# Sparse attention and FFN: the sparse units of each batch's last group take 128 rows instead of 64

## The chip, the cores and the metric

The kernel runs on one core of one Trainium2 chip. The metric is the device time of one execution in microseconds (us). Three executions of the kernel before took 803.14, 804.76 and 806.10 us; the median, 804.76 us, stands for it.

## The reference

Block-sparse attention for 4 batches, 8 heads, 768 positions and head size 64 is followed by a feed-forward net on 3072 tokens of width 512 with 2048 hidden units, all in float32. A query block of 32 positions sees its neighbours, the first and the last key block and three sampled blocks; the first and the last query block see every key.

```python
scores = scale * np.matmul(q, k.transpose(0, 1, 3, 2))
mask = np.abs(blk_i - blk_j) <= window            # blocks of 32, window 1
mask = mask | (blk_i == 0) | (blk_j == 0) | (blk_i == n_blocks - 1) | (blk_j == n_blocks - 1)
for qb in range(n_blocks):
    for kb in sampled_blocks[qb]:
        mask[qb * block:(qb + 1) * block, kb * block:(kb + 1) * block] = True
scores = np.where(mask, scores, -1000000000.0)
attn = np.exp(scores - np.max(scores, axis=-1, keepdims=True))
attn = attn / (np.sum(attn, axis=-1, keepdims=True) + 1e-09)
out = np.matmul(attn, v)

h = x @ w_in                                      # x: the attention's output, 3072 x 512
g = np.maximum(h, 0.0) + np.log1p(np.exp(-np.abs(h)))
return g @ w_out
```

## The kernel before

**Attention.** The 24 query blocks of a batch are dealt into 6 groups of 4 blocks, in the order 1 to 23 and then 0. In the last group only blocks 21 and 22 are sparse; 23 and 0 see every key and form a *whole* set of their own. A batch is so 7 sets (`sets`): five sparse ones, the whole one, and the sparse one of the last group, which comes last. A set is two units (`units`), `a` = 0 and 1, each with two head pairs `j`; a pair is the heads `r` = 0 and 1, which lie in the two halves of the partitions of `q` and `k`. In all there are 56 units, of which 8 are sparse units of a last group.

A sparse unit runs through these stages. `scores` multiplies each of the `ni` query blocks (4, in the last group 2) with its 8 gathered key blocks (256 columns): query block `i` writes the 32 rows from 32*i of the PSUM tile `s` (L622), and DVE scales, masks and takes the row maximum, one instruction per head (L628). `exponents` is one ScalarE activation per head with its row sum (L678). `transposes` turns the probabilities on TensorE in chunks of 128 columns (L691) and copies them out of PSUM, one copy per four chunks, on ScalarE and VectorE (L698, L696). `values` multiplies with the gathered values, query block by query block, 32 rows of the PSUM tile `x` at a time (L721). After a set's second unit `normalise` divides by the row sums (L749 to L751), and `turn` transposes the result on TensorE (L766), from where ScalarE writes the rounded part (`x_high`, L780) and VectorE the rest (`x_low`, L784) into the FFN's input. With `ni` = 2 the score rows, the activations, the transposes and the products use 64 of the 128 rows.

**FFN.** It runs in two phases. Phase 0 takes hidden slices 0 to 5 for 8 blocks of 384 tokens and is mixed into the attention: `hidden` (L255 to L257, 12 products of 384 columns), the softplus on ScalarE and VectorE, `project` (L313 to L315, 9 products of 512 columns). Phase 1 takes slices 6 to 15 for 6 blocks of 512 tokens after the attention.

**Order.** The program lists the pieces of the attention and of the FFN in a fixed interleaving (`pieces`, `due`), in which a unit's scores stand two units ahead of its values. SyncE keeps that order. The other engines' queues are ordered by a list scheduler which works from the program's dependencies and its own estimates; each engine then works through its queue in order. Key blocks are gathered by GpSimd, VectorE and ScalarE copies (`kg`, L530, L516, L497) out of one batch's keys `kT`, which the next batch's replace once the whole set's scores have been taken; GpSimd also starts the indirect loads of sampled values (L588) and adds up the FFN's weights (L187).

## Time and profile before

| | |
|---|---|
| device time, three executions | 803.14, 804.76, 806.10 us (median 804.76) |
| span of the profiled execution, first to last instruction | 802.7 us (its own device time is not listed apart) |
| TensorE matmul busy | 775.1 us, 97% |
| TensorE weight loads | 612.0 us, 76% |
| VectorE busy | 529.6 us, 66% |
| ScalarE busy | 534.1 us, 67% |
| GpSimd busy | 217.2 us, 27% |
| last transposes of the attention | 418 us after the start |

Rows of the timeline give start and duration in us, the engine (PE is TensorE's products, DVE VectorE, ACT ScalarE, POOL GpSimd), the line, the operation, out<-in, and how many instructions the row sums up; in square brackets stands the idle time ahead of the row with what ended it. Neighbouring products overlap, so the cost of a row on TensorE is read from its start to the start of the next row, not from its duration. A product of two float32 operands leaves two records, which is why 8 products of L622 are listed as x16; a transpose leaves one.

### The profile page before, as it was taken

The numbers are of one execution on the slowest core, as the hardware profiler recorded it, in microseconds if no ns is written. First come the engines' busy times: TensorE is split into PE (matmuls) and PEld (weight loads), VectorE is DVE, ScalarE is ACT, GpSimd is POOL, SyncE is SP. The second block draws the span as 40 slices with busy tenths as digits, with TensorE's granted clock in tenths as the row PEclk, the third lists the DMA queues.
The fourth block names the chain that finished last, engine by engine and source line by source line (L and its number), as shares of the span: only waits on it lengthen the run. The fifth ranks groups of instructions, "written<-read, shape, count | busy, mean of one in ns | idle before, by whom it ended". The sixth has DMA issues, their size and how long they took to land.

```text
span 802.7 us, 20684 instructions
## 1 busy us (share of the span) xinstructions
PE 775.1 (97%) x7868; PEld 612.0 (76%) x7868; DVE 529.6 (66%) x1266; ACT 534.1 (67%) x1210; POOL 217.2 (27%) x389
## 2 busy tenths in 40 slices
PE   8779999999999999999999999999999999999997
PEld 8556777877777777787788888888888888888886
DVE  5779998888768768785656765454454544644544
ACT  5878997778777777777666775555555555555552
POOL 6864886526456355552000000000000000000000
PEclk9999999999999999999999999999999999999999
DMA  8899998877986976856315950320330412300301
GB/s 250 246 237 320 250 265 225 263 249 237 226 283 193 292 254 189 243 168 220 121 41 185 311 186 2 105 105 1 105 105 17 139 56 92 118 1 1 105 0 53
DMA packets 59731, 129.60 MB, mean 161 GB/s; under 512 B 5553, under 2 KB 17969, under 8 KB 58609
## 3 DMA queue, kind: packets, MB, share of 16 engines
q1 hardware_dynamic: 53632, 109.79, 44.2%
q0 software_dynamic: 5712, 17.57, 7.9%
q8 instruction: 62, 1.02, 0.5%
q10 hardware_dynamic: 288, 0.93, 0.3%
q14 instruction: 37, 0.29, 0.1%
HBM read 97.85 MB, written 30.41 MB: 160 GB/s over the span
## 4 chain that ended last, share of the span: by engine, by line
PE 68%; DVE 13%; ACT 11%; DMA 4%; issue 3%; SPq 1%; POOL 0%; POOLq 0%; DVEq 0%; ACTq 0%
PE h L255 9%; PE o L313 9%; PE h L256 9%; PE h L257 9%; PE o L314 9%; PE o L315 9%; ACT pr L678 4%; PE x L721 3%; PE t L691 3%; PE s L622 3%; DVE pr L628 2%; PE warm L853 2%; DVE e L268 2%; DVE wt L183 1%; DMA x<-xD 1%
## 5 line engine op out<-in xcount | busy, mean ns | idle before, releaser
L268 DVE SCALAR_TENSOR_TENSOR e<-u,e 128x512 f32<-128x512 f32 (+1 forms) x108 | 76.2, 705 | 184.5 <-ACT u L266 184.2
L255 PE MATMUL h<-x,w 128*128 128x512 f32 (+1 forms) x432 | 163.4, 378 | 3.2 <-DVE e L269 2.3
L256 PE MATMUL h<-x,w 128*128 128x512 f32 (+1 forms) x432 | 159.2, 369 | 0.0
L257 PE MATMUL h<-x,w 128*128 128x512 f32 (+1 forms) x432 | 159.0, 368 | 0.0
L313 PE MATMUL o<-w,gh 128*128 128x512 f32 x384 | 155.6, 405 | 0.0
L314 PE MATMUL o<-w,gh 128*128 128x512 f32 x384 | 152.5, 397 | 0.0
L315 PE MATMUL o<-w,gl 128*128 128x512 f32 x384 | 151.8, 395 | 0.0
L259 ACT ACTIVATE e<-h 128x512 f32<-128x512 f32 (+1 forms) x108 | 59.2, 548 | 132.2 <-PE h L257 132.0
L678 ACT ACTIVATE pr<-pr,nmax 128x256 f32<-128x256 f32 (+2 forms) x208 | 110.0, 530 | 30.7 <-DVE nmax L628 18.5
L588 POOL DMA_INDIRECT vg<-in_v_dram,ix x88 | 87.9, 998 | 73.7 <-PE x L721 43.1
L255 PEld LDWEIGHTS h<-x,w 128*128 128x128 f32 x432 | 81.1, 188 | 20.5 <-DVE e L269 2.9
L530 POOL COPY kg<-kT 128x128 f32 x252 | 84.8, 381 | 43.9 <-PE s L622 41.1
L313 PEld LDWEIGHTS o<-w,gh 128*128 128x128 f32 x384 | 72.1, 188 | 24.8 <-issue 8.6
L257 PEld LDWEIGHTS h<-x,w 128*128 128x128 f32 x432 | 81.2, 188 | 10.7
L256 PEld LDWEIGHTS h<-x,w 128*128 128x128 f32 x432 | 81.3, 188 | 10.5
L283 ACT CAST gh<-u 128x512 fp32r<-128x512 f32 (+1 forms) x108 | 61.5, 569 | 41.5 <-PE o L314 41.1
L315 PEld LDWEIGHTS o<-w,gl 128*128 128x128 f32 x384 | 72.1, 188 | 17.7 <-issue 0.4
L314 PEld LDWEIGHTS o<-w,gh 128*128 128x128 f32 x384 | 72.2, 188 | 16.2 <-issue 0.8
L274 ACT ACTIVATE u<-u 128x512 f32<-128x512 f32 (+1 forms) x108 | 62.9, 582 | 24.8 <-DVE e L268 24.6
L628 DVE CUSTOM_DVE_ANT_1 pr<-s,mask 128x256 f32<-128x256 f32 (+1 forms) x192 | 69.4, 414 | 6.4 <-PE s L622 6.4
L289 DVE TENSOR_TENSOR gl<-u,gh 128x512 fp32r<-128x512 f32 (+1 forms) x108 | 70.1, 649 | 4.9 <-ACT gh L283 4.5
L279 DVE TENSOR_TENSOR u<-u,e 128x512 f32<-128x512 f32 (+1 forms) x108 | 69.8, 646 | 3.5 <-ACT u L274 1.6
(81 smaller groups left out, 1072.3 us busy)
## 6 DMA issues: line engine op xcount, KB each, us to landing
vg<-in_v_dram SPq DMA_DIRECT2D x19, 768.0 KB, 6.8
xD<-x SPq DMA_DIRECT2D x8, 1536.0 KB, 11.1
raw<-in_w_in_dram SPq DMA_DIRECT2D x16, 512.0 KB, 10.7
raw<-in_w_out_dram SPq DMA_DIRECT2D x16, 512.0 KB, 10.4
qc<-in_q_dram SPq DMA_DIRECT2D x24, 256.0 KB, 8.7
vg<-in_v_dram SPq DMA_DIRECT2D x12, 512.0 KB, 4.7
yD<-os SPq DMA_DIRECT2D x24, 256.0 KB, 3.0
x<-xD SPq DMA_DIRECT2D x4, 1536.0 KB, 8.3
```

Of the source, the lines that this page charges most:

```text
L255: nc.tensor.matmul(ph, wh[:, cols], hi[:, c], start=(c == 0), stop=False)
L256: nc.tensor.matmul(ph, wh[:, cols], lo[:, c], start=False, stop=False)
L257: nc.tensor.matmul(ph, wl[:, cols], hi[:, c], start=False, stop=(c == NC - 1))
L268: nc.vector.scalar_tensor_tensor(out=e, in0=u, scalar=-1.0, in1=e, op0=ALU.add, op1=ALU.subtract)
L289: nc.vector.tensor_tensor(out=gl, in0=l, in1=G[n].bitcast(F32), op=ALU.subtract)
L313: nc.tensor.matmul(po[m], gh[:, cols], wh, start=first, stop=False)
L314: nc.tensor.matmul(po[m], gh[:, cols], wl, start=False, stop=False)
L315: nc.tensor.matmul(po[m], gl[:, cols], wh, start=False, stop=last)
L530: copy(out=kd[:, i, 1 + NR + s, :], in_=kT[b][:, bass.ds(x, 1), :].rearrange("p n f -> p (n f)"))
L588: nc.gpsimd.indirect_dma_start(out=vd[0 : 3 * BLOCK, 1, i, :], out_offset=None, in_=v, in_offset=bass.IndirectOffsetOnAxis(ap=ix[:, b, 4 * ...
L628: nc.vector.tensor_tensor_reduce(out=pr[r][rows, j], in0=ps[r][rows, j], in1=mask[rows, g].unsqueeze(2).to_broadcast([ni * BLOCK, NS, BLOCK]),
L678: nc.scalar.activation(x, x, AF.Exp, bias=nmax[rows, r, j : j + 1], scale=-1.0, accum_out=rs[rows, h : h + 1])
```

## The change

The two head pairs of a unit in the last group are laid under each other: pair `j`, query block `i` takes the 32 rows from 32*(2*j + i). What was two tiles of 64 rows per head becomes one of 128.

- `scores`: the same 8 products per unit, now on four bands of 32 rows instead of two; two masked row maxima of 128 x 256 instead of four of 64 x 256.
- `exponents`: two activations of 128 x 256 instead of four of 64 x 256.
- `transposes`: four of 128 x 128 instead of eight of 64 rows, into one PSUM tile instead of two, and one copy of 128 x 512 (ScalarE) instead of two of 128 x 256.
- `values`: the same 16 products per unit, on four bands instead of two, in the order r, c, j, i instead of j, r, c, i.
- `normalise`: 128 x 256 instead of 64 x 512; `turn`: two transposes of 128 rows instead of four of 64.
- once, ahead of the loop: the mask's rows of the last group are copied from rows 0 to 63 to rows 64 to 127 on VectorE.

```diff
+    def folded(g, whole):
+        return whole or g == NG - 1
 ...
-        if not whole:
+        if not whole and g == NG - 1:
             gathered(key_work, place[b, g])
             kd = kg[place[b, g] % 2]
-            ni = NI if g < NG - 1 else 2
+            ps = [ps_s.tile([P, NS, BLOCK], F32, tag="s", name=f"s{n}_{r}") for r in range(2)]
+            for j in range(2):
+                p = 2 * a + j
+                cols = slice(p * BLOCK, (p + 1) * BLOCK)
+                for i in range(2):
+                    at = (2 * j + i) * BLOCK
+                    for r in range(2):
+                        half = slice(64 * r, 64 * r + 64)
+                        nc.tensor.matmul(
+                            ps[r][at : at + BLOCK], qd[half, p, i, :], kd[half, i, :, cols],
+                            start=True, stop=True,
+                        )
+            for r in range(2):
+                nc.vector.tensor_tensor_reduce(
+                    out=st["pr"][r][:, 0 : NS * BLOCK].rearrange("p (s k) -> p s k", s=NS), in0=ps[r],
+                    in1=mask[:, g].unsqueeze(2).to_broadcast([P, NS, BLOCK]),
+                    scale=-SCALE, scalar=BIG, op0=ALU.add, op1=ALU.min, accum_out=nmax[:, r, 0:1],
+                )
+            st["rows"] = P
+            st["chunks"] = 2
 ...
-            if whole:
-                parts = [(st["pr"][r], 0, 2 * a + r)]
+            if folded(g, whole):
+                parts = [(st["pr"][r][:, 0 : st["chunks"] * P], 0, 2 * a + r)]
 ...
+        if not whole and g == NG - 1:
+            for r in range(2):
+                at = (2 * a + r) * D
+                for c in range(2):
+                    for j in range(2):
+                        h = 2 * (2 * a + j) + r
+                        for i in range(2):
+                            rows = slice((2 * j + i) * BLOCK, (2 * j + i + 1) * BLOCK)
+                            nc.tensor.matmul(
+                                xq[rows, at : at + D], pt[r, c][:, rows],
+                                vd[:, c, i, h * D : (h + 1) * D], start=(c == 0), stop=(c == 1),
+                            )
 ...
-        for p in range(NA if whole else NP):
-            nc.tensor.transpose(ps[:, p, 0:rows], xs[0:rows, p * P : (p + 1) * P], ident[0:rows, 0:rows])
+        for p in range(NA if folded(g, whole) else NP):
+            nc.tensor.transpose(ps[:, p], xs[:, p * P : (p + 1) * P], ident)
 ...
     scores(0)
+    nc.vector.tensor_copy(out=mask[2 * BLOCK : P, NG - 1], in_=mask[0 : 2 * BLOCK, NG - 1])
```

The queues move at three places that the prediction speaks of. In the new program the lines are numbered anew: L622 is L649 for an ordinary unit and L624 for a folded one, L721 is L748, L691 is L718, L766 is L804, L780 is L819, L678 is L705 and L628 is L655. In the rows, `s` are scores, `pr` probabilities, `t` and `pt` their transposes, `x` the products with the values or the FFN's input, `h` and `o` the FFN's products.

TensorE's queue around the first folded unit's values in the third batch, before:

```order
L766 MATMUL y_5334<-ident,xs_5255 128x128 x2
L721 MATMUL x_5337<-vg_173,pt_0_5260 32x64 x4
L721 MATMUL x_5337<-vg_173,pt_4_5267 32x64 x4
L721 MATMUL x_5337<-vg_173,pt_0_5260 32x64 x4
L721 MATMUL x_5337<-vg_173,pt_4_5267 32x64 x4
L313 MATMUL o_0_5368<-w_1452,gh_5122 128x512
```

and now:

```order
L804 MATMUL y_5272<-ident,xs_5200 128x128 x2
L748 MATMUL x_5275<-vg_173,pt_0_5205 32x64 x16
L313 MATMUL o_0_5306<-w_1453,gh_5071 128x512
L314 MATMUL o_0_5306<-w_1454,gh_5071 128x512
L315 MATMUL o_0_5306<-w_1453,gl_5137 128x512
```

The 16 products stay at their place between the same neighbours; they now read one transposed tile instead of two.

ScalarE's queue at the start of the last group of the third batch, before:

```order
L274 ACTIVATE u_5043<-u_5043 128x384
L283 CAST gh_5122<-u_4896 128x384
L678 ACTIVATE pr_0_5057,sums_5079<-pr_0_5057,nmax_5056 64x256 x2
L678 ACTIVATE pr_1_5058,sums_5079<-pr_1_5058,nmax_5056 64x256 x2
L497 COPY kg_178<-kT_4949 128x4x128 x2
L780 CAST x_5_4857<-y_5084 128x4x128
L259 ACTIVATE e_5138<-h_5125 128x384
```

and now:

```order
L274 ACTIVATE u_4996<-u_4996 128x384
L283 CAST gh_5071<-u_4849 128x384
L819 CAST x_5_4810<-y_5033 128x4x128
L705 ACTIVATE pr_0_5010,sums_5030<-pr_0_5010,nmax_5009 128x256
L705 ACTIVATE pr_1_5011,sums_5030<-pr_1_5011,nmax_5009 128x256
L497 COPY kg_178<-kT_4902 128x4x128 x2
L259 ACTIVATE e_5087<-h_5074 128x384
```

Besides the two activations that are gone, the cast of the preceding set's result into `x` has moved from behind the activations and the copies of the next batch's keys to ahead of them. The second batch's queue changes in the same way.

VectorE's queue at the program's start, where the first unit's masked maxima stand, before:

```order
L530 COPY kg_178<-kT_189 128x128
L628 ISA pr_0_317,nmax_316<-s_0_319,mask 128x256
L628 ISA nmax_316 128x1
L628 ISA pr_0_317,nmax_316<-s_0_319,mask 128x256
L628 ISA nmax_316 128x1
L628 ISA pr_1_318,nmax_316<-s_1_320,mask 128x256
L628 ISA nmax_316 128x1
L628 ISA pr_1_318,nmax_316<-s_1_320,mask 128x256
L628 ISA nmax_316 128x1
L516 COPY kg_179<-kT_189 128x4x384
```

and now:

```order
L530 COPY kg_178<-kT_189 128x128
L903 COPY mask<-mask 64x8
L516 COPY kg_179<-kT_189 128x4x384
L655 ISA pr_0_317,nmax_316<-s_0_319,mask 128x256
L655 ISA nmax_316 128x1
L655 ISA pr_0_317,nmax_316<-s_0_319,mask 128x256
```

The mask's copy stands ahead of the first unit's maxima, and with it the large copy of the second group's keys (L516), which used to stand behind them.

More of the change, by code (lines that the diff above doesn't have):

```diff
@@ L608, in scores @@
         st["pr"] = [wk.tile([P, S], F32, tag="pr", name=f"pr{n}_{r}", bufs=4) for r in range(2)]
-        if not whole:
+        if not whole and g == NG - 1:
             gathered(key_work, place[b, g])
             kd = kg[place[b, g] % 2]
-            ni = NI if g < NG - 1 else 2
+            ps = [ps_s.tile([P, NS, BLOCK], F32, tag="s", name=f"s{n}_{r}") for r in range(2)]
[18 more added lines that the diff above has]
+            st["chunks"] = 2
+        elif not whole:
+            gathered(key_work, place[b, g])
+            kd = kg[place[b, g] % 2]
+            ni = NI
             rows = slice(0, ni * BLOCK)
@@ L711, in values @@
         xq = xps[m]
-        if not whole:
-            ni = NI if g < NG - 1 else 2
+        if not whole and g == NG - 1:
[7 more added lines that the diff above has]
+                            nc.tensor.matmul(
+                                xq[rows, at : at + D],
+                                pt[r, c][:, rows],
+                                vd[:, c, i, h * D : (h + 1) * D],
+                                start=(c == 0), stop=(c == 1),
+                            )
+        elif not whole:
             for j in range(2):
@@ L718, in values @@
                     for c in range(2):
-                        for i in range(ni):
+                        for i in range(NI):
                             rows = slice(i * BLOCK, (i + 1) * BLOCK)
@@ L744, in normalise @@
         xq, rs = xps.pop(m), sums.pop(m)
-        rows = P if whole or g < NG - 1 else 2 * BLOCK
-        n = NP if whole else 2 * NP
+        n = NP if folded(g, whole) else 2 * NP
         xs = xss[m] = wk.tile([P, DM], F32, tag="xs", name=f"xs{m}")
-        rs = rs[0:rows, 0:n]
+        rs = rs[:, 0:n]
         nc.vector.tensor_scalar_add(out=rs, in0=rs, scalar1=1e-9)
@@ L751, in normalise @@
         nc.vector.tensor_tensor(
-            out=xs[0:rows, 0 : n * D].rearrange("p (n d) -> p n d", n=n),
-            in0=xq[0:rows, 0 : n * D].rearrange("p (n d) -> p n d", n=n),
-            in1=rs.unsqueeze(2).to_broadcast([rows, n, D]), op=ALU.mult,
+            out=xs[:, 0 : n * D].rearrange("p (n d) -> p n d", n=n),
+            in0=xq[:, 0 : n * D].rearrange("p (n d) -> p n d", n=n),
+            in1=rs.unsqueeze(2).to_broadcast([P, n, D]), op=ALU.mult,
         )
@@ L762, in turn @@
         xs = xss.pop(m)
-        rows = P if whole or g < NG - 1 else 2 * BLOCK
         ps = ps_s.tile([P, NP, P], F32, tag="s", name=f"y{m}")
-        for p in range(NA if whole else NP):
-            nc.tensor.transpose(ps[:, p, 0:rows], xs[0:rows, p * P : (p + 1) * P], ident[0:rows, 0:rows])
+        for p in range(NA if folded(g, whole) else NP):
+            nc.tensor.transpose(ps[:, p], xs[:, p * P : (p + 1) * P], ident)
         t, at = divmod(place[b, g], GROUPS)
@@ L769, in turn @@
             x_tile(t)
-        if whole:
-            hi, lo = (X[0, t][:, i, :, at * P + 64 : (at + 1) * P] for i in range(2))
+        if folded(g, whole):
+            at = at * P + (64 if whole else 0)
+            hi, lo = (X[0, t][:, i, :, at : at + 64] for i in range(2))
             src = ps[:, 0:NA].rearrange("p a (o t) -> p (a o) t", o=2)
         else:
-            hi, lo = (X[0, t][:, i, :, at * P : at * P + rows] for i in range(2))
-            src = ps[:, :, 0:rows]
+            hi, lo = (X[0, t][:, i, :, at * P : (at + 1) * P] for i in range(2))
+            src = ps
         turned[m] = (hi, lo, src)
```

## The prediction

> **What bounds the kernel now.** I read the page's engine totals first, then a table of stretches, then TensorE's timeline where the changed units run.
>
> ```profile
> span 802.7 us, 20684 instructions
> PE 775.1 (97%) x7868; PEld 612.0 (76%) x7868; DVE 529.6 (66%) x1266; ACT 534.1 (67%) x1210; POOL 217.2 (27%) x389
> ```
>
> The stretches that follow are the last groups of the four batches with their neighbours (82:112, 185:225, 290:326, 395:425) and a piece of the FFN alone (480:600); the columns are the busy time of each engine, the granted clock and the DMA engines' share.
>
> ```profile
> 82.00:112.00 30.00, 27.38 (x436) 21.24 (x435) 29.14 (x75) 28.12 (x78) 25.22 (x45) 1.00 1.03 239
> 185.00:225.00 40.00, 38.96 (x529) 29.57 (x528) 32.73 (x89) 32.02 (x87) 22.94 (x53) 1.00 0.84 238
> 290.00:326.00 36.00, 34.26 (x506) 26.34 (x498) 28.65 (x73) 27.29 (x74) 24.23 (x47) 1.00 0.76 220
> 395.00:425.00 30.00, 29.77 (x369) 24.57 (x358) 16.04 (x50) 18.76 (x49) 1.82 (x2) 1.00 0.17 54
> 480.00:600.00 120.00, 120.00 (x517) 96.88 (x516) 60.05 (x94) 65.33 (x109) 0.00 (x0) 1.00 0.21 71
> ```
>
> In the first batch VectorE (29.14 of 30 us) and ScalarE (28.12) have no room left, and TensorE waits for them. In the second and third TensorE is busy for 97% and 95% of the stretch, VectorE for 82% and 80%. In the fourth TensorE has 0.23 us idle in 30 and the others are a little over half busy. After that the FFN alone keeps TensorE busy without a gap, so what the attention saves is not taken back by a wait behind it. The clock is 1.00 everywhere here.
>
> **The products.** The rows are TensorE's timeline; start to next start is the cost.
>
> ```profile
> 139.59 1.09 PE L622 MATMUL s<-kg,qc 64*32 64x256 f32 x32
> 140.61 0.50 PE L313 MATMUL o<-w,gh 128*128 128x512 f32 x1
> 143.35 1.10 PE L721 MATMUL x<-vg,pt 128*32 128x64 f32 x64
> 144.39 1.09 PE L691 MATMUL t<-ident,pr 128*128 128x128 f32 x8
> 145.23 0.42 PE L255 MATMUL h<-x,w 128*128 128x384 f32 x1
> 393.10 1.52 PE L646 MATMUL s<-kT,qc 64*64 64x384 f32 x16
> 394.55 1.10 PE L721 MATMUL x<-vg,pt 128*32 128x64 f32 x64
> 402.62 0.60 PE L766 MATMUL y<-ident,xs 128*128 128x128 f32 x4
> 403.15 1.62 PE L735 MATMUL x<-vg,pt 128*64 128x64 f32 x48
> 408.25 1.07 PE L622 MATMUL s<-kg,qc 64*32 64x256 f32 x16
> 409.24 1.62 PE L735 MATMUL x<-vg,pt 128*64 128x64 f32 x48
> 413.72 0.44 PE L766 MATMUL y<-ident,xs 128*128 128x128 f32 x2
> 413.91 0.42 PE L255 MATMUL h<-x,w 128*128 128x384 f32 x1
> 417.54 0.71 PE L691 MATMUL t<-ident,pr 64*128 64x64 f32 x8
> 418.18 0.49 PE L313 MATMUL o<-w,gh 128*128 128x512 f32 x1
> 420.48 1.09 PE L721 MATMUL x<-vg,pt 128*32 128x64 f32 x32
> 421.49 0.44 PE L255 MATMUL h<-x,w 128*128 128x384 f32 x1
> 423.78 0.46 PE L766 MATMUL y<-ident,xs 64*128 64x64 f32 x4
> 424.17 0.50 PE L313 MATMUL o<-w,gh 128*128 128x512 f32 x1
> ```
>
> *Scores.* An ordinary unit's 32 records take 1.02 us (139.59 to 140.61), a last group's 16 take 0.99 (408.25 to 409.24): half the work in the same time. The ordinary unit writes four bands of rows from two halves of the contraction, eight places in all, the last group four, so both have four records one after the other per place, and that sets the time. L646 has four in turn too, but 384 columns each: 1.45 us (393.10 to 394.55). The 128 further columns cost 0.46, 0.115 per record, so 256 columns cost 0.23 and four in turn 0.92, which leaves 0.07 to 0.10 as a constant. After the change the 16 records have eight places and two in turn: 0.46 and 0.09, 0.55 us. Saved 0.44 per unit; the ends are 0 (the places do not help) and 0.50 (half).
>
> *Values.* Likewise 64 records on four bands take 1.04 us (143.35 to 144.39), 32 on two bands 1.01. Halving the turns leaves 0.5 to 0.6; I take 0.56, saved 0.45, with ends 0 and 0.51.
>
> [...] The rows above show a constant beside the turns, so the sum stays with the rows.
>
> *Transposes.* Eight of 64 rows take 0.64 us (417.54 to 418.18), eight of 128 rows 0.84 (144.39 to 145.23), so four of these take 0.42; by L766, where four take 0.53 (402.62 to 403.15), they take 0.53. Saved 0.11 to 0.22, I take 0.2. *Turn.* Four of 64 rows take 0.39 (423.78 to 424.17), two of 128 took 0.19 (413.72 to 413.91); next to another kind of product, half of 0.53. Saved 0.1 to 0.2, I take 0.1 per batch.
>
> A batch has two such units: 2 x (0.44 + 0.45 + 0.2) + 0.1 = 2.28 us of TensorE, with ends 2 x 0.11 + 0.1 = 0.3 and 2 x (0.50 + 0.51 + 0.22) + 0.2 = 2.7.
>
> **VectorE and ScalarE.** These are the groups by form; the columns after the count are total us and mean ns.
>
> ```profile
> L628 DVE CUSTOM_DVE_ANT_1 pr<-s,mask 128x256 f32<-128x256 f32 x160 | 57.9, 416 | 6.4 <-PE s L622 6.4
> L628 DVE CUSTOM_DVE_ANT_1 pr<-s,mask 64x256 f32<-64x256 f32 x32 | 11.5, 409 | 0.0
> L678 ACT ACTIVATE pr<-pr,nmax 128x256 f32<-128x256 f32 x160 | 79.2, 497 | 12.5 <-DVE nmax L628 12.4
> L678 ACT ACTIVATE pr<-pr,nmax 64x256 f32<-64x256 f32 x32 | 15.9, 500 | 6.2 <-DVE nmax L628 6.0
> L698 ACT COPY pt<-t 128x512 f32<-128x512 f32 x76 | 41.8, 578 | 1.2 <-PE t L691 1.0
> L698 ACT COPY pt<-t 128x256 f32<-128x256 f32 x12 | 4.1, 363 | 0.0
> L696 DVE COPY pt<-t 128x256 f32<-128x256 f32 x4 | 1.6, 412 | 0.0
> L751 DVE TENSOR_TENSOR xs<-x,sums 128x256 f32<-128x256 f32 x4 | 1.6, 408 | 0.0
> L751 DVE TENSOR_TENSOR xs<-x,sums 64x512 f32<-64x512 f32 x4 | 2.7, 675 | 0.2 <-PE x L721 0.2
> ```
>
> A maximum or an activation over 64 rows takes as long as one over 128 (409 against 416 ns, 500 against 497), so each one removed counts in full. Per batch VectorE loses four maxima (11.5 us over 32 instances, 0.36 each: 1.44), one copy (0.41) and 0.27 in L751: 2.1 us. ScalarE loses four activations (2.0); its copies go from 0.363 to 0.578 in the first unit and from twice 0.363 to 0.578 in the second, 0.07 more in all: 1.9 us. All three engines thus shed about 2 us per batch at the same place, so no engine becomes the bound that was not.
>
> **What lands.** *First batch:* TensorE waits there for the other two, so their saving counts, the smaller 1.9, and TensorE's own only shortens its work ahead of a wait. One ordinary unit behind it gets its scores listed as five and five instead of in turns (a few tenths on TensorE, covered by the same wait). I take 1.7; the ends are 0.3 and 2.1. *Second and third:* 2.28 each, by the TensorE share of 97% and 95%; since waits of a microsecond stand in these stretches, some of the time saved becomes a longer wait, and I take 85%: 3.9. The ends are 0.6 and 5.4. *Fourth:* nothing to wait for, 2.3; ends 0.3 and 2.7.
>
> *The moved cast.* In the third batch TensorE stood still for it:
>
> ```profile
> 300.19 0.57 ACT L780 CAST x<-y 128x512 fp32r<-128x512 f32 x1
> 301.54 0.66 PE L691 MATMUL t<-ident,pr 128*128 128x128 f32 x4 [1.04 <-DVE x L784]
> ```
>
> The transposes waited 1.04 us for VectorE's L784, which needs ScalarE's cast; the cast stood behind the activations and key copies. It now stands ahead. What is late next is the group's own activations, by the cast's 0.57 us. I take half, 0.5; the ends are 0 and 1.0. In the second batch, where the cast moves in the same way, I count nothing:
>
> ```profile
> 189.92 3.77 DVE L516 COPY kg<-kT 128x1536 f32<-128x1536 f32 x1
> 298.10 0.94 DVE L516 COPY kg<-kT 128x1536 f32<-128x1536 f32 x1
> ```
>
> there VectorE itself was held by a key copy of 3.77 us, four times that of the third batch.
>
> *The start.* The mask's copy of 8 columns, which costs no more than the 0.41 us of L696's 256, and L516 now come ahead of the first maxima.
>
> ```profile
> 16.51 0.42 DVE L628 CUSTOM_DVE_ANT_1 pr<-s,mask 128x256 f32<-128x256 f32 x1 [1.51 <-PE s L622]
> ```
>
> VectorE stood idle for 1.51 us there, waiting for TensorE; 0.41 + 0.94 = 1.35 fit in. If L516 took 3.77 instead, the first maxima would be 2.7 us late. I take 0, with ends -0.9 (the copy no longer stands between the first two units) and +2.7. No DMA is added or moved, and SyncE's queue keeps its order.
>
> Sum: 1.7 + 3.9 + 2.3 + 0.5 = 8.4 us. The profiled span of 802.7 becomes 794.3. The median of the runs is 2.1 above that span, for the work around it and the spread; carried over, 804.76 - 8.4 = 796.4 us.
>
> **Rivals.**
>
> *The time saved turns into waits.* In the first three batches the chain from the preceding set, the key copies and the cast decides, and TensorE only arrives earlier. For it: the waits quoted, and TensorE's 27.38 of 30 in the first. Against: VectorE and ScalarE shorten by as much. Then only the fourth batch's 2.3 and half a microsecond count: 802.0 us, within what a measurement tells from no change (0.5% here, 4 us).
>
> *The bands do not run beside each other,* so the change does not do what it says on TensorE: scores and values stay at 0.99 and 1.01. Then 0.5 per batch is left in the last three batches (1.5) and the first batch's 1.7: 804.76 - 3.2 = 801.6. Against: the ordinary units' 32 and 64 records in the same time, in the same mode.
>
> *Key copies collide with GpSimd's.* VectorE's maxima end earlier, so L516 starts earlier and may run wholly beside GpSimd's gather of the same keys. The row at 189.92 prices a copy in such company at 3.77 instead of 0.94, 2.83 more. There are two at each of three batch changes and one at the start. From three further copies at that price on the path (8.5) the gain is gone; with five of the seven, 14.2, the time is 804.76 - 8.4 + 14.2 = 810.6, slower. Against: in the stretches concerned VectorE has 7 us free per batch, which would cover most of it. [...]
>
> **How the numbers follow.** The forecast has 0.72, waits 0.13, bands 0.07, collisions 0.05, and 0.03 is left for a reordering that none of these names. Faster by over 0.5% is below 800.7: the forecast less 0.01 for its upper edge, 0.03 of the bands' case, which ends close to that bound, and 0.01 of the rest: 0.75. Within 0.5% come the waits with 0.13, 0.04 of the bands, and 0.01 each of the edge and the rest: 0.19. Slower are the collisions and 0.01 of the rest: 0.06. The forecast's own range is from all the high ends, 2.1 + 5.4 + 2.7 + 1.0 + 0.9 = 12.1 (792.7), to a sum of 4 (800.8). The range given goes from 792.0, this low end with some of the runs' own spread, to 802.5, which takes in the two cases that end at 802.
>
> **What would show it.** Right: in the new profile a last group's scores (x16) take 0.55 us to the next start and its values (x32) 0.56, four transposes 0.4 to 0.5; 16 maxima and 16 activations fewer; the wait of 1.04 us gone; the attention's last transposes 8 us earlier and the FFN after them unchanged in length. Wrong: the same start to start as before (bands); the rows shorter but TensorE's waits in 185:225 and 290:326 longer by as much (waits); more L516 rows near 3.8 us (collisions); a first maximum later than 16.5 us.

## The result and the profile after

Eight executions of the changed kernel took 795.72 to 800.69 us, median 799.73; eight of the kernel before, on the same chip, 800.79 to 806.10, median 804.69. The ratio is 0.9934 with a 95% interval of 0.9908 to 0.9961: faster by 0.66%, about 5 us, where 8.4 were forecast; the median lies inside the range given, 792.0 to 802.5. The profiled span went from 802.7 to 797.5 us.

The totals of the profile after:

```profile
span 797.5 us, 20516 instructions
PE 768.4 (96%) x7828; PEld 605.4 (76%) x7828; DVE 528.9 (66%) x1231; ACT 528.3 (66%) x1174; POOL 216.4 (27%) x389
```

TensorE's busy time fell by 6.7 us and the span by 5.2. The same stretches as before the change, by engine, with the granted clock, the DMA share and GB/s at the end:

```profile
82.00:112.00 30.00, 25.29 (x378) 17.78 (x374) 28.53 (x64) 24.72 (x63) 25.24 (x45) 0.94 1.04 231
185.00:225.00 40.00, 36.16 (x506) 27.28 (x506) 30.07 (x70) 27.97 (x72) 20.57 (x46) 0.91 0.75 206
290.00:326.00 36.00, 33.81 (x541) 26.19 (x540) 29.89 (x67) 27.57 (x70) 22.93 (x47) 1.00 0.84 232
395.00:425.00 30.00, 29.84 (x329) 25.45 (x328) 14.73 (x37) 18.98 (x45) 1.07 (x2) 1.00 0.29 99
480.00:600.00 120.00, 120.00 (x518) 96.84 (x517) 59.70 (x93) 65.25 (x109) 0.00 (x0) 1.00 0.22 71
```

The third to fifth rows look as forecast. The first two do not: TensorE is busy for 25.29 instead of 27.38 us and for 36.16 instead of 38.96, and the granted clock, which was 1.00 in both, is 0.94 and 0.91.

**The products themselves did what was forecast.** TensorE's timeline in the fourth batch, start to next start:

```profile
406.20 0.66 PE L624 MATMUL s<-kg,qc 64*32 64x256 f32 x16
406.79 1.62 PE L775 MATMUL x<-vg,pt 128*64 128x64 f32 x48
410.54 0.60 PE L718 MATMUL t<-ident,pr 128*128 128x128 f32 x4
410.97 0.38 PE L804 MATMUL y<-ident,xs 128*128 128x128 f32 x2
412.04 0.65 PE L748 MATMUL x<-vg,pt 128*32 128x64 f32 x32
412.63 0.45 PE L256 MATMUL h<-x,w 128*128 128x384 f32 x1
419.55 0.38 PE L804 MATMUL y<-ident,xs 128*128 128x128 f32 x2
419.69 0.48 PE L313 MATMUL o<-w,gh 128*128 128x512 f32 x1
```

Scores 0.59 us (0.99 before, 0.55 forecast), transposes 0.43 (0.64 before, 0.42 forecast), values 0.59 (1.01 before, 0.56 forecast). That is about 1.03 us per unit and 2.1 per batch, and 2.3 with the turn's 0.25 (0.39 before, 0.14 now), where 2.28 were counted. The other engines by form:

```profile
L655 DVE CUSTOM_DVE_ANT_1 pr<-s,mask 128x256 f32<-128x256 f32 x160 | 57.9, 416 | 4.1 <-PE s L649 4.1
L629 DVE CUSTOM_DVE_ANT_1 pr<-s,mask 128x256 f32<-128x256 f32 x16 | 6.2, 418 | 3.8 <-PE s L624 3.8
L705 ACT ACTIVATE pr<-pr,nmax 128x256 f32<-128x256 f32 x176 | 87.3, 498 | 12.2 <-DVE nmax L655 10.6 <-DVE nmax L629 1.2
L516 DVE COPY kg<-kT 128x1536 f32<-128x1536 f32 x20 | 30.5, 1523 | 0.0
```

There are 16 maxima and 16 activations fewer, at an unchanged duration each (416 and 418 ns after 416 and 409, and 498 after 497 and 500). But the 20 large key copies of L516 took 30.5 us instead of 25.9.

**Where the rest went.** In the second batch (GpSimd, VectorE and TensorE in the timeline of after, then two stretches of it):

```profile
187.23 4.33 POOL L530 COPY kg<-kT 128x128 f32 x18
191.53 1.27 POOL L187 TENSOR_TENSOR wt<-wt,raw 128x512 int32<-128x512 int32 x1
187.66 5.96 DVE L516 COPY kg<-kT 128x1536 f32<-128x1536 f32 x1
193.54 0.68 DVE L823 TENSOR_TENSOR x<-y,x 128x512 fp32r<-128x512 f32 x1
194.27 1.11 PE L718 MATMUL t<-ident,pr 128*128 128x128 f32 x4 [3.19 <-DVE x L823]
```

```profile
190.00:195.00 5.00, 1.80 (x14) 1.53 (x13) 5.00 (x4) 2.04 (x5) 2.80 (x8) 0.81 0.38 98
195.00:200.00 5.00, 5.00 (x27) 3.01 (x25) 2.78 (x9) 2.58 (x7) 1.82 (x6) 0.51 0.11 40
```

The key copy for the next batch takes 5.96 us beside a row of GpSimd copies (3.77 before); L823, which stands behind it in VectorE's queue, comes late, TensorE waits 3.19 us, and then runs at a clock of 0.51 for 5 us, which costs some 2.5 us more (an estimate: half of the 5). The wait is nearly paid a second time. In the kernel before the same wait was 0.84 us:

```profile
194.34 0.66 PE L691 MATMUL t<-ident,pr 128*128 128x128 f32 x4 [0.84 <-DVE x L784]
```

In the third batch it is milder: a copy of 4.53 us (0.94 before) and a wait of 1.62 (1.04 before), with the clock at 1.00:

```profile
297.15 4.53 DVE L516 COPY kg<-kT 128x1536 f32<-128x1536 f32 x1
302.32 0.66 PE L718 MATMUL t<-ident,pr 128*128 128x128 f32 x4 [1.62 <-DVE x L823]
```

In the first batch another VectorE instruction takes longer beside GpSimd, the weight conversion L177 (2.18 us; the same instruction took 0.41 and 0.42 in this stretch before). The copy of a transposed tile, L723, stands behind it now, TensorE waits 2.95 us and the clock falls to 0.77:

```profile
104.26 1.30 POOL L187 TENSOR_TENSOR wt<-wt,raw 128x512 int32<-128x512 int32 x1
103.67 2.18 DVE L177 TENSOR_SCALAR wt<-wt 128x512 int32<-128x512 int32 x1
106.85 0.68 DVE L723 COPY pt<-t 128x512 f32<-128x512 f32 x1
107.58 0.58 PE L804 MATMUL y<-ident,xs 128*128 128x128 f32 x2 [2.95 <-DVE pt L723]
105.00:110.00 5.00, 2.42 (x67) 1.94 (x67) 5.00 (x8) 1.66 (x4) 2.77 (x3) 0.77 1.08 197
```

Before, L723's counterpart L696 stood ahead of L177:

```profile
106.48 0.67 DVE L696 COPY pt<-t 128x512 f32<-128x512 f32 x1
107.08 0.41 DVE L177 TENSOR_SCALAR wt<-wt 128x512 int32<-128x512 int32 x1
```

**The ledger.** TensorE runs the FFN's hidden blocks in the same order in all these kernels, so the start of the same L255 product in two profiles tells how far one is ahead of the other. The stages are bounded by the first hidden block, the ninth (behind the first batch's last group), the 21st, the 33rd and the 47th. Minus is gained. "Here" is the chip of the result and others on which the kernel before takes 803 to 805 us; "second chip" is one on which it takes 816 to 818 and reaches its first hidden block at 68.76 us instead of 59.63. Each kernel is set against the one profile of the kernel before from its group of chips. The rows hold one execution each; the kernels are those of the experiments below.

| kernel | start | 1st batch | 2nd | 3rd | 4th | phase 1 | span |
|---|---|---|---|---|---|---|---|
| change, here | -2.55 | +0.97 | +2.88 | -2.98 | -2.80 | -0.69 | -5.2 |
| change, second chip | -1.13 | +2.05 | +1.41 | -1.29 | -2.90 | +0.50 | -1.3 |
| values two bands at a time, second chip | -1.11 | +3.95 | -1.67 | -1.34 | -2.87 | +0.02 | -3.0 |
| fourth batch alone, second chip | -1.53 | -0.17 | -0.16 | +1.16 | -2.89 | +0.01 | -3.6 |
| change, key copy on ScalarE, second chip | +0.56 | -0.56 | -1.31 | -1.89 | -2.77 | +0.32 | -5.6 |
| change, key copy late, second chip | -0.16 | +0.34 | -1.30 | -1.77 | -2.77 | +0.06 | -5.6 |
| before, key copy on ScalarE, second chip | -2.16 | +0.39 | +0.44 | +0.90 | +0.04 | -0.41 | -0.8 |
| before, mask's copy alone, second chip | -0.33 | +0.06 | +1.03 | +1.12 | +0.02 | -0.37 | +1.5 |
| change, both copies on ScalarE, here | -1.13 | +2.77 | -1.68 | -4.41 | -2.72 | -0.31 | -7.5 |
| change, the one copy on ScalarE, here | -2.54 | +2.95 | +3.25 | -4.23 | -2.81 | -0.71 | -4.1 |
| before, both copies on ScalarE, here | -0.63 | +0.93 | +0.03 | -0.55 | +0.01 | -0.37 | -0.6 |
| last three batches, key copy on ScalarE, here | -1.02 | +2.08 | -1.73 | -3.12 | -2.84 | -0.77 | -7.4 |

A stage whose code is unchanged differs by up to about 1 us between two executions (the 1.16 in the row of the fourth batch alone), the start by 2, so only larger differences, or ones that recur, say anything. In the third stage the second chip's profile of the kernel before is itself short: 108.41 us, where the five other profiles without the new form in the third batch have 109.31 to 109.91. The second chip's gains there look up to 1 us too small.

### The profile page after: what moved, and what is told of

Read it like the earlier page. It is cut to its first block, busy times and chain, and to the rows that moved or that the text cites. A ratio compares the mean times of both kernels' runs of the same rounds, so it can differ in the third digit from the quotient of the medians.

```text
span 797.5 us, 20516 instructions
## 1 busy us (share of the span) xinstructions
PE 768.4 (96%) x7828; PEld 605.4 (76%) x7828; DVE 528.9 (66%) x1231; ACT 528.3 (66%) x1174; POOL 216.4 (27%) x389
## 4 chain that ended last, share of the span: by engine, by line
PE 66%; DVE 16%; ACT 11%; DMA 4%; issue 2%; SPq 0%; ACTq 0%; DVEq 0%
PE o L313 10%; PE o L314 10%; PE o L315 10%; PE h L255 9%; PE h L256 9%; PE h L257 9%; ACT pr L705 4%; PE t L718 2%; DVE pr L655 2%; DVE kg L516 2%; DMA vg<-in_v_dram 2%; PE x L761 2%; PE s L649 2%; DVE e L268 2%; DVE wt L183 1%
## 5 line engine op out<-in xcount | busy, mean ns | idle before, releaser
L268 DVE SCALAR_TENSOR_TENSOR e<-u,e 128x512 f32<-128x512 f32 (+1 forms) x108 | 76.7, 711 | 178.9 <-ACT u L266 178.8
L255 PE MATMUL h<-x,w 128*128 128x512 f32 (+1 forms) x432 | 163.2, 378 | 1.7 <-DVE e L269 0.9
L705 ACT ACTIVATE pr<-pr,nmax 128x256 f32<-128x256 f32 (+1 forms) x192 | 102.2, 534 | 24.3 <-DVE nmax L686 12.0
L255 PEld LDWEIGHTS h<-x,w 128*128 128x128 f32 x432 | 81.1, 188 | 19.3 <-DVE nmax L680 2.2
L289 DVE TENSOR_TENSOR gl<-u,gh 128x512 fp32r<-128x512 f32 (+1 forms) x108 | 69.4, 642 | 5.6 <-ACT gh L283 5.6
L279 DVE TENSOR_TENSOR u<-u,e 128x512 f32<-128x512 f32 (+1 forms) x108 | 69.6, 644 | 3.0 <-ACT u L274 1.6
L718 PE MATMUL t<-ident,pr 128*128 128x128 f32 x448 | 63.1, 280 | 7.9 <-DVE x L823 4.8
```

The lines of the kernel that those rows point to most:

```text
L255: nc.tensor.matmul(ph, wh[:, cols], hi[:, c], start=(c == 0), stop=False)
L268: nc.vector.scalar_tensor_tensor(out=e, in0=u, scalar=-1.0, in1=e, op0=ALU.add, op1=ALU.subtract)
L279: nc.vector.tensor_tensor(out=l, in0=l, in1=e, op=ALU.add)
L705: nc.scalar.activation(x, x, AF.Exp, bias=nmax[rows, r, j : j + 1], scale=-1.0, accum_out=rs[rows, h : h + 1])
L718: nc.tensor.transpose(ps[:, i, 0:rows], st["pr"][r][0:rows, c * P : (c + 1) * P], ident[0:rows, 0:rows])
```

## The experiments

Theory: each batch saves some 2 us of TensorE; in the second and third batch the key copy on VectorE gives part or all of it back, because it meets GpSimd's copies; in the first, VectorE's queue does the same. Rival: saved time turns into waits wherever it is saved, and the copy only happened to be the last of them. The start's 2.55 us are the change's, or an accident.

### The key copy on ScalarE

```diff
-                ins = nc.vector.tensor_copy(
+                ins = (nc.scalar.copy if g == 0 and b > 0 else nc.vector.tensor_copy)(
                     out=kd[:, 0:ni, 0:NR, :]...                       # L516
```

> The changed kernel, with one move: in the second, third and fourth batch the copy of the local key blocks for the batch's first group (the L516 copy that took 5.96 us in the second batch and 4.53 us in the third, beside GpSimd's 18 copies) runs on ScalarE and no longer on VectorE. Theory (the saving of the change was eaten because VectorE was held by that copy, so that the low part of the attention result came 3.19 and 1.62 us late for TensorE, and TensorE's clock then fell to 0.51 for 5 us): both waits and the clock drop go; the second batch gives back about 3.2 + 2.2 us, the third 1.6, less about 1 us each for what ScalarE now has more; 794 to 797, that is 3 to 5 below the changed kernel's 799.7. Rival (the saved TensorE time turns into waits on VectorE and ScalarE wherever it is saved, and the copy only happened to be the last of them): another wait takes its place, 799 to 801.

Measured, on the second chip: 808.26 us against 817.70, ratio 0.9866 (0.9824 to 0.9907). The changed kernel itself had 0.9944 (0.9919 to 0.9969) there (below). That is 0.0078, or 6.4 us, below the changed kernel, more than the 3 to 5 expected, though from four executions only; the medians put it at 4.3 (9.4 below the kernel before, against 5.1). The copy on ScalarE takes 1.48 us, is done before GpSimd's copies begin, and L823 is no longer held:

```profile
195.40 1.48 ACT L516 COPY kg<-kT 128x1536 f32<-128x1536 f32 x1
198.84 5.32 POOL L530 COPY kg<-kT 128x128 f32 x18
200.99 0.67 DVE L823 TENSOR_TENSOR x<-y,x 128x512 fp32r<-128x512 f32 x1
```

In the ledger the second batch turns from a loss of 1.4 into a gain of 1.3. The granted clock stays at 1.00 from 195 to 215 us. The rival falls for the second batch. In the third the gain grows by 0.6 us only, which is within the scatter. The first batch differs as well (+2.05 against -0.56), though no key copy was held there, so not all of the gain belongs to the move.

### The key copy late on VectorE

```diff
-            if i == 0:
+            if i == (ni - 1 if g == 0 and b > 0 else 0):
                 at = kT[b][:, 4 * g : 4 * g + NR, :]                  # and L516 under it
```

> The changed kernel, with the same copy left on VectorE but emitted with the last of the group's four key blocks and not with the first, so that it stands behind the subtraction for which TensorE waited, and behind the two masked maxima of the last unit. Theory: the subtraction comes on time, and the waits of 3.19 and 1.62 us and the clock drop go, as with the copy on ScalarE; if the copy still meets GpSimd's copies it holds VectorE later, in front of the scores that need it, which may cost 1 to 2 us in each of two batches; 794 to 799. Rival (saved time turns into waits in any case): 799 to 801.

Measured, on the same chip: 809.90 us, ratio 0.9892 (0.9852 to 0.9932). The copy is back on VectorE and takes 0.96 us, 12 us later than in the first experiment:

```profile
207.85 0.96 DVE L516 COPY kg<-kT 128x1536 f32<-128x1536 f32 x1
```

So it is not the copy's own work on VectorE that costs, but its place: 0.96 us here, 5.2 in the changed kernel on this chip. In the third batch another VectorE instruction ran beside GpSimd's row of key copies instead, L183, for 3.27 us instead of 0.69; TensorE then waited 0.48 us for L823.

```profile
307.30 3.27 DVE L183 SCALAR_TENSOR_TENSOR wt<-raw,wt 128x512 int32<-128x512 int32 x1
```

The two ways of clearing the place agree in the ledger to 0.2 us in the second, third and fourth batch.

### The same move in the kernel before

The edit of the first experiment, in the kernel before.

> The kernel before, with the same move of the L516 copy to ScalarE in the first group of batches two to four. Theory: of the three copies only the second batch's was held there (3.77 us, the others 0.94), and TensorE lost little by it; 0 to 1.5 us below before's time, so the gain by the same edit is at least twice as large in the changed kernel. Rival (the copy is a burden on VectorE at any time, apart from the meeting with GpSimd): the same 3 to 5 us as in the changed kernel.

Measured: 817.46 us, ratio 0.9990 (0.9964 to 1.0017). Nothing that can be told, as the theory has it: the move is worth 4 to 6 us in the changed kernel and 0.8 in the one before (3 at the end of the interval). What it takes back is a loss that the change made.

### The mask's copy alone

```diff
     scores(0)
+    nc.vector.tensor_copy(out=mask[2 * BLOCK : P, NG - 1], in_=mask[0 : 2 * BLOCK, NG - 1])
```

> The kernel before, with only the change's one new line outside the last groups: the copy of half of the mask's last column after the first unit's scores, whose result nothing uses here. It costs VectorE one small copy, and it moves the key copy of the second group ahead of the first masked maxima in VectorE's queue. Theory (the 2.55 us by which the changed kernel starts its first feed-forward products earlier come from that order at the start, and from the clock that then doesn't fall): 2 to 3 us below before's time, with granted clock 1.00 from 25 to 35 us. Rival (the start of before's profiled run was bad luck, or the gain comes from the first batch's last group): within 0.7 us of before's time.

Measured: 816.32 us, ratio 0.9984 (0.9962 to 1.0006). The line changes VectorE's queue at the start as the change does, and gains nothing that can be told: 1.3 us by the ratio, with an interval that still reaches the theory's 2 to 3. The profile speaks against the theory: the granted clock is 0.71 from 25 to 30 us, not 1.00. Over six profiles with that order on the second chip, the first hidden block starts 1.53 us earlier to 0.56 later than in the kernel before, and with the old order and the key copy moved 2.16 earlier. On the chips here four profiles with the new order start it at 57.08 to 58.62 us and two with the old at 59.01 and 59.63; the mean clock up to there is 1.00, 1.00, 0.97 and 0.97 against 0.91 and 0.94. Whether part of the 2.55 belongs to the change is open.

### The changed kernel and the kernel before, once more

> The changed kernel itself, once more, on the chip on which the next kernels run, as their base: the first two profiles were taken on another chip than the first four experiments, whose kernels all reached their first feed-forward product at 66.6 to 69.3 us, and not at 57.1 or 59.6. Theory (the copy of the local keys meets GpSimd's copies in the second and third batch because TensorE's saved time moves them together): the L516 copy takes over 3 us again in at least one of these two batches, and TensorE waits over 1.5 us for the subtraction behind it. Rival (the long copy was an accident of one execution): under 2 us in both. On the start: if the 2.55 us gained there belong to the change, this kernel's first product is again 2 to 3 us earlier than that of the kernel before, below; if they were an accident of the executions, the difference is anything.

> The kernel before, once more, for its profile on this chip. It should show the second batch's L516 copy at 2 us or more and the others near 0.95, and the first feed-forward product 2 to 3 us after that of the changed kernel if the start's gain belongs to the change.

Measured, on the second chip: 810.69 us against 815.78, ratio 0.9944 (0.9919 to 0.9969), the same gain as on the first chip. The long copies recur: 5.22 us in the second batch (2.97 in the kernel before) and 3.70 in the third (0.95 before). The second batch of the changed kernel:

```profile
201.36 5.22 DVE L516 COPY kg<-kT 128x1536 f32<-128x1536 f32 x1
207.24 0.94 PE L718 MATMUL t<-ident,pr 128*128 128x128 f32 x4 [2.42 <-DVE x L823]
205.00:210.00 5.00, 2.76 (x22) 1.52 (x23) 4.05 (x6) 1.93 (x5) 0.95 (x2) 0.75 0.02 8
```

It was no accident of one execution. In the third batch TensorE waited 0.96 us behind the copy of 3.70, against 0.69 in the kernel before, so there the copy cost little. The first feed-forward product is 1.13 us earlier, not 2 to 3. The profiled spans of this pair lie only 1.3 us apart where the medians lie 5.1 apart: the changed kernel's ten executions reach from 807.1 to 815.2, and the profiled one, with 814.25, is the second longest.

### The new form in the fourth batch alone

```diff
+    FOLDED = (B - 1,)
-    def folded(g, whole):
-        return whole or g == NG - 1
+    def folded(b, g, whole):
+        return whole or (g == NG - 1 and b in FOLDED)
```

(with `folded(b, g, whole)` in the places where the change asks for `g == NG - 1`, and the old code for the other batches)

> The changed kernel with its new form in the fourth batch's last group alone; the first three batches' last groups are computed as before the change, with 64 rows. Theory (in the first and second batch the saved time was lost again behind VectorE, in the third and fourth it stayed): it keeps the fourth batch's 2.2 to 2.8 us, and so lies 2 to 3 us below before (beyond whatever the start gives, which its profile shows), that is no more than 1 us behind the changed kernel with four batches in the new form. Rival (each batch gives about the same, 2 us): 2 us below before and 4 to 6 us behind the changed kernel.

Measured, on the second chip: 812.20 us, ratio 0.9951 (0.9928 to 0.9974), against the changed kernel's 0.9944. A quarter of the change gives all but 0.6 us of the whole by the ratios, all but 1.5 by the medians. It lies 3.6 us below before by the medians, a little more than the theory's 2 to 3. The ledger has 2.89 us for the fourth batch, and the other batches within the scatter. In this kernel the second batch's key copy runs beside the same 18 GpSimd copies and is not held:

```profile
197.57 5.43 POOL L530 COPY kg<-kT 128x128 f32 x18
199.31 0.95 DVE L516 COPY kg<-kT 128x1536 f32<-128x1536 f32 x1
```

GpSimd's copies take 5.43 us here and 4.33 where VectorE was held; one of the 18 took 1.42 us, the others 0.28 to 0.29. So where the two met, the longer time was on VectorE in one profile (5.96 instead of 0.95) and on GpSimd in the other (1.42 instead of 0.28).

### The values' products two bands at a time

```diff
-                for c in range(2):
-                    for j in range(2):
+                for j in range(2):
+                    for c in range(2):
                         h = 2 * (2 * a + j) + r
```

> The changed kernel with the values' products of the new form in another order: for each 64 columns both chunks of the one head pair first and then those of the other, so that two neighbouring products in four, and not four, go to different bands of output rows. Theory (the values got from 1018 to 584 ns because four bands run beside each other): 0.85 to 1.05 us for 32 such products, 0.3 to 0.45 us more in each of eight units, 2.4 to 3.6 us behind the changed kernel where nothing hides it. Rival (products to different bands overlap however they are ordered, the queue looks far enough ahead): 0.58 us as now, and the same time.

Measured, on the second chip: 811.28 us, ratio 0.9952 (0.9930 to 0.9975), not to be told from the changed kernel. One of its units' values, start to next start:

```profile
425.03 0.68 PE L748 MATMUL x<-vg,pt 128*32 128x64 f32 x32
425.64 0.45 PE L256 MATMUL h<-x,w 128*128 128x384 f32 x1
```

0.61 us against 0.59, not 0.85 to 1.05; of the eight units seven have 0.61 and one 0.84. The rival's time holds; whether the queue looks ahead, as it has it, no row shows. The time that the change saves goes with how many bands the 16 products use (1.01 us on two, 0.59 on four), and hardly with the order in which they are issued (0.61).

This kernel's profile tells something else besides. Its key copies met GpSimd's too, for 3.66 us in the second batch and 3.65 in the third, yet the second batch gained 1.67 us:

```profile
203.32 3.66 DVE L516 COPY kg<-kT 128x1536 f32<-128x1536 f32 x1
207.63 0.66 PE L718 MATMUL t<-ident,pr 128*128 128x128 f32 x4 [0.88 <-DVE x L823]
```

TensorE waited 0.88 us here, and 2.42 behind the copy of 5.22 in the changed kernel. Over all profiles it waited 0.78 to 0.96 us behind the six held copies of 2.84 to 3.77 us, about as long as behind one of 0.95 in the kernel with the fourth batch alone (0.82), and 1.62 to 3.19 behind the four of 4.53 to 5.96. So a held copy did not cost by itself; the cost came with the four long ones. The first batch lost 3.95 us here.

### One more copy moved: the first batch

```diff
-            if n_ % 2 and not (units[n][1] and nch <= 4):
+            if n_ % 2 and not (units[n][1] and nch <= 4) and sets[units[n][0]] != (1, 0, False):
                 nc.vector.tensor_copy(...)                            # L723, else ScalarE's L725
```

> The changed kernel with the first groups' key copy on ScalarE (as in the first experiment) and, besides, one single copy more moved from VectorE to ScalarE: that of the second half of the transposed exponentials of the second batch's first unit, which stands behind a weight conversion of 2.2 us on VectorE and for which TensorE waited 2.55 to 2.95 us in three profiles, right after the first batch's last group. Theory (the first batch lost its saving to that queue on VectorE): the wait goes, the first batch's last group ends 1 to 2.5 us earlier, and the whole lies 1 to 2.5 us below the kernel with the key copy moved, that is at a ratio of 0.984 to 0.986 of before. Rival (VectorE is full in the first batch, and the next thing that it makes late, the feed-forward's chain of L268, L279 and L289, takes the wait over): within 0.7 us of the kernel with the key copy moved, 0.986 to 0.988.

> The kernel before, with both copies moved to ScalarE. Theory: neither of the two waits is long there, so the two moves bring nothing without the change, 0 to 1 us, ratio 0.998 to 1.0. Rival (they are a gain by themselves): 3 to 6 us, ratio below 0.996.

> The changed kernel with only the copy of the second batch's first unit moved to ScalarE, the key copy being left on VectorE. Theory: it takes 1 to 2.5 us off in the first batch, and the second and third batch lose as before behind the key copy (over 3 us in one of them at least): 1 to 2.5 us below the changed kernel, ratio 0.991 to 0.993. Rival (the wait is taken over): the changed kernel's 0.994.

All three ran on one chip, with the kernel before at 803.85 us. Measured: with both copies moved 799.82, ratio 0.9955 (0.9931 to 0.9978); in the kernel before 802.90, 0.9994 (0.9976 to 1.0013); with the one copy alone 802.03, 0.9976 (0.9957 to 0.9994). The kernel before behaves as its theory has it. The other two miss both their theories and their rivals: 0.9955 is above 0.984 to 0.988, and 0.9976 above 0.991 to 0.994, so a ratio like the key copy's 0.9866 did not recur on this chip. Between the two, the key copy's move turns the second batch from +3.25 to -1.68 in the ledger, and the medians by 2.2 us. The theory fails for the first batch. The wait goes at its place and comes back at the next one, the FFN's chain on VectorE: in the kernel with both copies moved, and in the one with this copy alone (TensorE's row and the stretch around it, each):

```profile
111.60 0.44 PE L255 MATMUL h<-x,w 128*128 128x384 f32 x1 [1.99 <-DVE e L269]
110.00:115.00 5.00, 3.40 (x12) 3.32 (x13) 5.00 (x16) 3.84 (x12) 0.43 (x2) 0.73 1.05 276
```

```profile
110.27 0.69 PE L255 MATMUL h<-x,w 128*128 128x384 f32 x1 [5.04 <-DVE e L269]
110.00:115.00 5.00, 4.73 (x20) 4.63 (x20) 5.00 (x14) 3.95 (x13) 1.45 (x1) 0.60 1.05 353
```

VectorE is busy for 5.00 of 5.00 us there in both. The first batch loses 2.8 and 3.0 us against the kernel before. The profiled execution with both copies moved gained 7.5 us, the median only 4: its twelve executions reach from 795.2 at a mean granted clock of 0.996 to 803.4, and those over 802 us all have 0.990 or less. In the kernel with the one copy alone the second batch's L516 took 5.94 us, the third's 1.08.

### The last three batches, and the key copy on ScalarE

`FOLDED = range(1, B)`, and the edit of the first experiment.

> The changed kernel with the new form in the last groups of the second, third and fourth batch alone, the first batch's last group being computed with 64 rows as before the change; and the first groups' key copy on ScalarE. Theory (in the first batch VectorE is busy without a break, so that TensorE's saved time piles up into one wait of 2.5 to 5 us, and the clock that falls after it makes the net a loss of 1 to 2.5 us; in the second and third batch the key copy on VectorE does the same, and with it moved each keeps 1.7 to 3.4 us; the fourth keeps 2.1 to 2.9): the first batch ends where before's does, no wait of TensorE over 1.7 us between 95 and 125 us and granted clock 1.00 there, and the whole lies 6 to 8.5 us below before, ratio 0.9895 to 0.9925. Rival (the waits belong to VectorE's load in every batch, and new ones come in the second and third): 3 to 5 us, ratio 0.994 to 0.996, as with the change itself and with both copies moved.

Measured, on another chip: 797.16 us against 803.26, ratio 0.9930 (0.9905 to 0.9956), a little less than the theory's 0.9895 to 0.9925. The first batch, not folded:

```profile
111.30 0.45 PE L255 MATMUL h<-x,w 128*128 128x384 f32 x1 [1.29 <-DVE e L269]
105.00:110.00 5.00, 4.61 (x111) 2.96 (x109) 5.00 (x9) 4.49 (x12) 4.84 (x9) 1.00 0.81 188
110.00:115.00 5.00, 3.71 (x30) 3.31 (x30) 5.00 (x16) 4.17 (x13) 2.78 (x3) 1.00 1.06 255
```

No long wait and a clock of 1.00, as expected; over the whole profile the mean clock is 0.998. But the first batch does not end where before's does: it comes 2.08 us later, of which the moved copy may make 0.9 (the kernel before with both copies moved has +0.93 there). So leaving the new form out of the first batch took away the wait and the slow clock, but not the late end. The second and third give 1.73 and 3.12. In microseconds it is the shortest median of these kernels, but on a chip of its own; its ratio is close to the 0.9934 of the change itself.

## Why the prediction was right in sign and too large

**The products** (2.28 us per batch): right, 2.3 measured. The constant ahead of the turns was a little larger than taken, 0.13 instead of 0.09 beside 0.46 for the scores; the turn saved more, 0.25 instead of 0.1. Half the time of before, the high end that the prediction allowed, would be 0.50 for the scores, and the rows have 0.59.

**The fourth batch** (2.3): right in kind and a little small, 2.7 to 2.9 in all nine profiles with the new form there, just above the high end of 2.7. The rows above account for 2.3 of it.

**VectorE and ScalarE** (2.1 and 1.9 us per batch): the instructions counted are gone, but VectorE's busy time fell by 0.7 us in all (529.6 to 528.9), not by 8.4. Its key copies took 4.6 us more and the weight conversions L177 1.7 more. ScalarE's fell by 5.8 (534.1 to 528.3), not by 7.6.

**The first batch** (1.7): no such gain, +1.0 and +2.1 in the two pairs, and from -0.56 to +3.95 over the seven profiles with the new form there. The step that failed is "TensorE waits there for the other two, so their saving counts". The queue on VectorE was put in another order, one of its instructions took 1.8 us longer beside GpSimd, and TensorE stood still in one wait of 2.95 us, after which the clock fell (0.66 over the next 5 us). Moving the first thing that was late only showed the next. That this is the cause of the loss is argued and not shown: with the new form left out of the first batch, the stage still ended 2.08 us late.

**The second batch** (half of 3.9, from 85% of the busy share): lost 2.88 and 1.41 us in the two pairs. The step that failed is "some of the time saved becomes a longer wait, and I take 85%", with the key copy taken to be as long as before. In the first pair the wait grew by 2.35 us (0.84 to 3.19) and the clock of 0.51 cost some 2.5 (an estimate, as above), 4.8 together, which is the distance from the forecast's 1.9 to the loss of 2.88. With the key copy out of the way it gained 1.3 to 1.7 in all four kernels. The rival of the key copies that collide was the one at work, priced at 2.83 us per collision and given 0.05. Its price was low, since the clock was not in it, and its reach was overrated: two copies of seven got longer, one of them held before already, and only one cost much. The argument against it, "VectorE has 7 us free per batch, which would cover most of it", failed because the free time lay elsewhere than in front of the one subtraction that TensorE waits for.

**The third batch** (the other half): gained 2.98 and 1.29, and 3.12 to 4.41 here and 1.34 to 1.89 on the second chip in the other kernels with the new form there; the second chip's numbers are up to 1 us too small, as said. That is about what was forecast or more, in spite of the held copies.

**The moved cast** (0.5 in the third batch, 0 in the second): wrong: the wait for L823 is longer, 1.62 us instead of 1.04, and not gone. The step that failed is that the cast's place decided this wait; VectorE was held by the key copy there too. With the key copy on ScalarE, or later on VectorE, no wait for L823 over 0.6 us is left in these two batches.

**The start** (0): open. The 2.55 us in the first pair of profiles, without which the span there would have fallen by 2.6, came once more here (2.54) and not on the second chip (from 1.53 earlier to 0.56 later).

**What was luck:** in the first pair the four batches together give 1.9 us where 8.4 were forecast; the start's 2.55 and phase 1's 0.69, for which the forecast had nothing, make the rest of the 5.2. The time came inside the range by these. The medians of both chips nevertheless agree on a gain of 5 us; one profile of each kernel, with a clock that differs from execution to execution (a mean of 0.988 to 0.993 in the eight of the changed kernel), doesn't give it to better than 2 or 3.

**What stays open:** how much the key copy's move is worth on the other chips. On the second chip it brought 4.3 to 6.4 us; where it was tried together with the other copy, on another chip, it brought 1.7 (0.9955 against 0.9976). Also why the first batch loses, why that of the last kernel ended 2 us late without the new form, and how much of the start belongs to the change.

## What to carry to other kernels

A saving on the busiest engine is worth what the engines beside it can follow, at the one instruction that it waits for next; a free share over 40 us says nothing about the queue in front of that instruction. Before such a change is made everywhere, make it in one place, the one without neighbours: here the last of four places gave 70% of the gain by the medians and nearly all of it by the ratios. And put a copy like L516, which took 0.94 to 1.14 us in most places and up to 5.96 beside GpSimd's row of copies, somewhere else than ahead of what the critical engine needs.

## What the runs showed of the hardware

In the two profiles of the first pair a VectorE copy of 1536 float32 columns (L516) took 0.94 to 1.14 us in 32 of 40 places, and 1.41 to 2.12 in five where it ran beside GpSimd's L187. Beside GpSimd's row of key copies it took 2.84 to 5.96 in ten cases of all the profiles. In six of the ten it ended 0.8 us after the last instruction of the row, which with the longest was the last of 19 that followed one on the other; in the other four it got in ahead of the last and took 2.84 to 3.77. In the kernel with the fourth batch alone it took 0.95, and one GpSimd copy took 1.42 instead of 0.28. Besides L516 and L177 (2.18 instead of 0.41), other VectorE instructions took longer in places where they met GpSimd's: in the first pair, with 384 columns, L268 up to 2.37 us, L279 up to 1.44 and L289 up to 1.65 (at most 0.56 where they met none of its instructions) and, with 512 columns, L183 3.27 in the second experiment (at most 0.70 in the first pair where it met none). L269, also with 384 columns, never took over 0.56 in the first pair, in 40 cases that met GpSimd's instructions too. Why these and not L269 is not shown. With the longest L516, GpSimd's 18 key copies follow one another every 0.24 us, each of 0.29 to 0.31, and L187 after them takes 1.27; the copy on VectorE ends 0.82 us after that, so its length was not that of any one instruction there.

The granted clock went with the length of a single wait of TensorE. Taken over the 5 us after each wait above 1.1 us between 70 and 420 us in all 14 profiles: after the 20 waits of 1.11 to 1.47 us it was 1.00; of the seven from 1.51 to 1.89 us, three left it at 1.00 and four brought it to 0.68 or 0.69; after each of the nine from 1.99 us up it was 0.50 to 0.66. By these shares the drop costs another 1.7 to 2.5 us (an estimate: 5 us at 0.66 to 0.50), so that here a wait of 2 to 3 us was paid nearly twice, and one of up to 1.47 only once.
